# Hedgehog attention: exponents of two heads' planes side by side, keys times values as whole matmuls

## The chip, the cores and the metric

One core of a Trainium2 chip. TensorE multiplies matrices into PSUM, VectorE (DVE), ScalarE (ACT) and GpSimd (POOL) work on tiles in SBUF and (the first two) in PSUM, SyncE (SP) issues most DMAs. The metric is the device time of one execution in microseconds, as the median of several runs.

## The reference, cut to what matters

The input x (2048 rows of 512) is layer-normalised. Two branches work on the result, and both are added to x: a linear attention of 32 heads of 16 features (A), and a dense layer pair with the Mish activation (B).

```python
pq = einsum("bhsd,hdf->bhsf", q, w_phi)          # 16 features per head
pk = einsum("bhsd,hdf->bhsf", k, w_phi)
phi_q = concat([softmax(pq), softmax(-pq)])      # two planes of 16
phi_k = concat([softmax(pk), softmax(-pk)])
kv  = einsum("bhsf,bhsd->bhfd", phi_k, v)        # keys times values, over all rows
z   = einsum("bhsf->bhf", phi_k)
num = einsum("bhqf,bhfd->bhqd", phi_q, kv)
den = einsum("bhqf,bhf->bhq", phi_q, z) + 1e-6
o   = num / den
return x + o @ wo + (h * tanh(softplus(h))) @ w2   # h = xn @ w1 + b1
```

## The kernel before

The 2048 rows are 16 tiles of 128, in four groups. All instructions are issued in the order in which the code calls them (a manual schedule); every engine works through its own queue in that order, and waits come from the tiles' dependencies and from the buffers of the pools.

**First phase, four stages** (the loop over `s`, L560 to L604). Stage `s` takes the exponentials of the keys of group `s` (`exponentials`, L249, ScalarE), multiplies the keys of group `s - 1` by their values (`accumulate`, L291, TensorE), projects the values of group `s` (`value`, L176; from stage 1 on the first two tiles are copied out by VectorE, the others by ScalarE) and the logits of step `s + 1` (`logits`, L211), normalises the keys' softmaxes (`normalise`, L268, VectorE), computes hidden units of the Mish layer (`hidden`, L185: four matmuls and one ScalarE activation each), and takes the next step's maxima and minima and subtracts them (`extremes`, L219, VectorE). In stage 2 the queries' weights are folded with w_phi (`fold`, L107: 16 matmuls, four copies). In stage 0, and at the start, the loads, the layer norms and the keys' fold come first.

The exponents of a step lie in the tile `e`: per row tile two planes (one for the softmax, one for that of the negated logits) of 512 columns, 32 heads of 16 features. L242 writes a plane.

`accumulate` multiplies 32 columns of `e` (two heads, one plane) by the 33 columns of `vext` that hold these two heads' values and a one. It puts four such matmuls side by side in the array, as column tiles: 128 matmuls a group, 512 in all, into one PSUM tile `pkv` of one bank. `mask_kv` (L310, VectorE) copies it to `kvm`, and clears what belongs to the other head of each pair. `masks` (L322, POOL) prepares the mask and the constant columns of `kvm`.

**Second phase** (L607 to L702). Steps 4 to 7 are the queries' groups. They are not normalised; each tile's exponents are transposed by a DMA on SP (`turn`, L258). `attend` (L334) multiplies a tile's transposed exponents by `kvm`: 32 matmuls as four row tiles, into the four banks of `pnd`; ScalarE copies the denominators to `ds` (L357) and the numerators (L363). `combine` (L365, VectorE) forms the quotients: L379, L382, L385 and L387 work on `ds`, L394 and L401 on the numerators, and a DMA on SP transposes the outcome. `second_layer` (L412) and `project_out` (L425) are the matmuls into the output tile `po` (L420, L429); `residual` (L435) adds x on VectorE (L437), and SP stores.

**PSUM.** The eight banks are shared by pools. `ps` has four buffers and stays open. In the first phase `px` (one) is open beside it, and from the end of stage 0 on `pk` (one bank, for `pkv`) and `pz` (two). Projections, folds and hidden units take their banks in turn from these pools (`bank`, L66); the list at L602 gives the order from the last four units of stage 0 on. A matmul that opens a tile waits until the bank's former tile has been copied out. Before `attend(0, 0)` the upper four banks are given back (L614) and become `pnd`.

Of the kernel before, what the change touches and what calls it, by code (L numbers as in the profile page):

```python
# [18 lines left out]
def kernel(  # L19
# [13 lines left out]
    P = 128  # L33
# [40 lines left out]
    x_sb = persist.tile([P, NT, D], BF16, name="x_sb")  # L74
    xnT = persist.tile([P, NT, KT, P], BF16, name="xnT")
    acts = persist.tile([P, FT, S], BF16, name="acts")
    kvm = persist.tile([P, 2, 4, 36], BF16, name="kvm")
    wqk = wts.tile([P, KT, 2 * D], BF16, name="wqk")
    wsrc = wts.tile([P, 4, DH], BF16, name="wsrc")
    wv = wts.tile([P, KT, D], BF16, name="wv")  # L80
# [26 lines left out]
    def fold(wT, dst, dve, kts=range(KT)):  # L107

        for kt in kts:
            pf = bank("pfold")  # L110
            for j in range(4):
                nc.tensor.matmul(
                    pf[:, j * P : (j + 1) * P],
                    lhsT=wT[:, j, kt * P : (kt + 1) * P],
                    rhs=Wbd[:, j, :],
                    start=True,
                    stop=True,
                )
            if kt in dve:
                nc.vector.tensor_copy(dst[:, kt, :], pf[:])  # L120
            else:
                nc.scalar.copy(dst[:, kt, :], pf[:])

    def ln_stats(t0, n):

# [93 lines left out]
    def extremes(s, between=None, halves=(slice(0, TPG),)):  # L219

        if s not in e_of:
            e_of[s] = epool.tile([P, TPG, 2, 512], BF16, name="e")
        for q in halves:
            n = q.stop - q.start
            e = e_of[s][:, q]
            pv = p_of[s][:, q, :].rearrange("p t (c e) -> p (t c) e", e=16)
            for pl, op in enumerate((ALU.max, ALU.min)):
                if pl == 1 and between is not None:
                    between()
                src = pv  # L230
                for half in (8, 4, 2):
                    m = smx.tile([P, 128, half], BF16, name=f"m{half}", bufs=1)[:, 0 : n * 32, :]
                    nc.vector.tensor_tensor(  # L233
                        out=m, in0=src[:, :, 0:half], in1=src[:, :, half : 2 * half], op=op
                    )
                    src = m

                m = smx.tile([P, 128, 1, 2], BF16, name="m1", bufs=1)[:, 0 : n * 32]
                nc.vector.tensor_tensor(out=m[:, :, 0, :], in0=src, in1=src[:, :, ::-1], op=op)
                mb = m.rearrange("p (t c) u o -> p t c u o", t=n).to_broadcast([P, n, 32, 8, 2])  # L240
                p5 = pv.rearrange("p (t c) (e o) -> p t c e o", t=n, o=2)
                nc.vector.tensor_tensor(  # L242
                    out=e[:, :, pl, :].rearrange("p t (c e o) -> p t c e o", e=8, o=2),
                    in0=p5 if pl == 0 else mb,
                    in1=mb if pl == 0 else p5,
                    op=ALU.subtract,
                )

    def exponentials(s, ks=(0, 1)):  # L249
        for k in ks:  # L250
            m = 2 if s < NG else 1
            for i in range(2 * k, 2 * k + 2, m):
                v = e_of[s][:, i : i + m, :, :]
                nc.scalar.activation(v, v, ACT.Exp)  # L254
                if s >= NG:
                    turn(s, k, i)

    def turn(s, k, i):  # L258

        h = 2 * (s - NG) + k  # L260
        if i == 2 * k:
            qT_of[h] = epool.tile([P, 2, 8, P], BF16, name="qT", bufs=3)
        nc.sync.dma_start_transpose(
            out=qT_of[h][:, i - 2 * k, :, :],
            in_=e_of[s][:, i, :, :].rearrange("p l c -> p (l c)"),
        )

    def normalise(s, k, between=None):  # L268

        v = e_of[s][:, 2 * k : 2 * k + 2, :, :]  # L270
        t = smx.tile([P, 128], FP32, name="s")
        nc.vector.reduce_sum(  # L272
            t[:], v.rearrange("p t l (c e) -> p (t l c) e", e=16), axis=AX.X
        )
        if between is not None:
            between()
# [4 lines left out]
        nc.vector.tensor_copy(  # L281
            r2[:], r[:].rearrange("p (c o) -> p c o", o=1).to_broadcast([P, 128, 2])
        )
        vv = v.rearrange("p t l (c e o) -> p (t l c) e o", e=8, o=2)
        nc.vector.tensor_tensor(  # L285
            out=vv, in0=vv, in1=r2[:, :, None, :].to_broadcast([P, 128, 8, 2]), op=ALU.mult
        )
# [2 lines left out]

    def accumulate(g, pk):  # L291
        if g == 0:
            kv_of[0] = pk.tile([P, 2, 4, 33], FP32, name="pkv", tag="kv")
        e = e_of.pop(g)
        for j in range(4):
            for pl in range(2):
                for i in range(TPG):
                    for r in range(4):
                        c = j * P + 32 * r
                        nc.tensor.matmul(  # L300
                            kv_of[0][32 * r : 32 * r + 32, pl, j, :],
                            lhsT=e[:, i, pl, c : c + 32],
                            rhs=vext[g % 2][:, i, j, r, 0:33],
                            start=(g == 0 and i == 0 and j == 0 and pl == 0),
                            stop=(g == NG - 1 and i == TPG - 1),
                            skip_group_check=True,
                            tile_position=(0, 32 * r),
                        )

    def mask_kv():  # L310
        kv = kv_of[0][:].rearrange("p l j c -> p (l j) c")
        to = kvm[:].rearrange("p l j c -> p (l j) c")
        nc.vector.tensor_tensor(
            out=to[:, :, 0:32], in0=kv[:, :, 0:32],
            in1=KVmask[:, None, 0:32].to_broadcast([P, 8, 32]), op=ALU.mult,
        )
        nc.vector.scalar_tensor_tensor(
            out=to[:, :, 32:34], in0=kv[:, :, 32:33].to_broadcast([P, 8, 2]), scalar=5e-7,
            in1=KVmask[:, None, 32:34].to_broadcast([P, 8, 2]), op0=ALU.add, op1=ALU.mult,
        )  # L320

    def masks():  # L322
        for r in range(4):
            rows, own = slice(32 * r, 32 * r + 32), block[32 * r : 32 * r + 32, 2 * r : 2 * r + 2, :]
            nc.gpsimd.tensor_copy(KVmask[rows, 0:32], own.rearrange("p h d -> p (h d)"))
            nc.gpsimd.tensor_copy(KVmask[rows, 32:34], own[:, :, 0])
            nc.gpsimd.tensor_copy(
                kvm[rows].rearrange("p l j c -> p (l j) c")[:, :, 34:36],
                own[:, None, :, 0].to_broadcast([32, 8, 2]),
            )  # L330

# [2 lines left out]
    def attend(h, i):  # L334

        if i == 0:
            nd_of[h] = (
                (wkp, wv)[h % 2][:].rearrange("p (i l) c -> p i l c", i=2),
                opool.tile([P, 2, 2, 64], FP32, name="ds"),
            )  # L340
        nm, ds = nd_of[h]
        pnd = later[0].tile([P, 4, 512], FP32, name="pnd", tag="nd")
        for pl in range(2):
            for j in range(4):
                for r in range(4):
                    at, rows = (pl * 4 + j) * 36, slice(32 * r, 32 * r + 32)
                    nc.tensor.matmul(  # L347
                        pnd[:, r, at : at + 36],
                        lhsT=qT_of[h][rows, i, pl * 4 + j, :],
                        rhs=kvm[rows, pl, j, :],  # L350
                        start=True,
                        stop=True,
                        tile_position=(32 * r, 0),
                    )
        a = pnd[:, :, 0:288].rearrange("p r (l j c) -> p l j r c", l=2, j=4)
        to = nm[:, i, :, :].rearrange("p l (j r c) -> p l j r c", j=4, r=4)
        nc.scalar.copy(  # L357
            ds[:, i].rearrange("p x (g r h) -> p g r x h", g=8, r=4),
            pnd[:, :, 0:288].rearrange("p r (g c) -> p g r c", g=8)[:, :, :, 32:36].rearrange(
                "p g r (x h) -> p g r x h", x=2  # L360
            ),
        )
        nc.scalar.copy(to, a[:, :, :, :, 0:32])  # L363

    def combine(h, parts=(slice(0, 2),)):  # L365

        nm, ds = nd_of.pop(h) if parts[-1].stop == 2 else nd_of[h]
        ds = ds[:].rearrange("p i x (l c) -> p i x l c", l=2)
        if h not in oT_of:
            ob = lnp.tile([P, 4, 512], BF16, name="ob", tag="xn")  # L370
            u = opool.tile([P, 2, 2, 32], FP32, name="u")
# [5 lines left out]
        for q in parts:  # L377
            n = q.stop - q.start
            nc.vector.tensor_tensor(  # L379
                out=u[:, q], in0=ds[:, q, 0], in1=ds[:, q, 1, ::-1], op=ALU.mult  # L380
            )
            nc.vector.tensor_tensor(  # L382
                out=w[:, q], in0=u[:, q, 0, :], in1=u[:, q, 1, :], op=ALU.add
# [2 lines left out]
            for k in range(q.start, q.stop):  # L386
                nc.vector.tensor_tensor(  # L387
                    out=f[:, k],
                    in0=ds[:, k, 1, ::-1, :, None].to_broadcast([P, 2, 32, 2]),
                    in1=w[:, k, None, :, None].to_broadcast([P, 2, 32, 2]),  # L390
                    op=ALU.mult,
                )
# [167 lines left out]
    for s in range(NG):  # L560
# [33 lines left out]
        if s == 0:  # L594
# [2 lines left out]
            wide = None  # L597
            stack.close()
            pk = upper.enter_context(tc.tile_pool(name="pk", bufs=1, space=PSUM))
            pz = upper.enter_context(tc.tile_pool(name="pz", bufs=2, space=PSUM))  # L600
            hidden(6)
            turns[0] = cycle([pz, ps, ps, pz, ps, px, ps])  # L602
        hidden((4, 14, 8, 10)[s])
        extremes(s + 1)  # L604

# [127 lines left out]
```

## Time and profile before

| what | us |
|---|---|
| median of three runs | 179.92 (179.86 to 179.94) |
| profiled execution | 179.79 |
| its span, first to last instruction | 177.7 |
| TensorE busy, matmuls | 171.8 |
| VectorE busy | 153.4 |
| ScalarE busy | 125.1 |
| start of `attend(0, 0)` | 101.33 |

The profiled execution is 2.1 us longer than its span, and 0.13 us shorter than the median. In the rows below, a line such as L300 is a line of the kernel before, PE is TensorE's matmuls and PEld its weight loads. Matmuls are pipelined, so a matmul's duration is longer than its share of the engine; the step from one start to the next tells the share. Times in lists count from the span's start.

```profile
L300 PE MATMUL pkv<-vext,e 128*32 128x33 bf16 x512 | 4.8, 184 | 0.0
L347 PE MATMUL pnd<-kvm,qT 32*128 32x36 bf16 x512 | 6.0, 174 | 0.2 <-DMA qT<-e 0.2
L313 DVE TENSOR_TENSOR kvm<-pkv,KVmask 128x256 bf16<-128x256 f32 x1 | 0.4, 417 | 0.0
L317 DVE SCALAR_TENSOR_TENSOR kvm<-pkv,KVmask 128x16 bf16<-128x16 f32 x1 | 0.2, 165 | 0.0
```

These are groups of equal instructions: line, engine, operation, output and inputs, shapes, count, then busy time in us, the mean duration in ns, and idle time before them with what ended it.

### The profile page before, as it was taken

Reading aid. Unit: us, or ns where it says so; the run is one execution under the profiler, and the core shown is the slowest. Engines: PE = TensorE matmul, PEld = TensorE weight load, DVE = VectorE, ACT = ScalarE, POOL = GpSimd, SP = SyncE. Lnnn points to the kernel's source line nnn. Section 1 sums busy time; section 2 is a strip of 40 time slices with the busy share of each in tenths; the row PEclk is TensorE's granted clock in tenths of the full one; section 3 lists DMA queues with packets and bytes.
Section 4 is the critical chain, followed back from the end, with each engine's and each line's share of the span. In section 5 each row is a group of like instructions: output and inputs, shape, how many; then the busy total and the mean of one; then the engine's idle time right before and its main releaser. Section 6 shows DMA issues by size and latency. Waiting matters only on the chain.

```text
span 177.7 us, 4351 instructions
## 1 busy us (share of the span) xinstructions
PE 171.8 (97%) x1806; PEld 81.7 (46%) x1806; DVE 153.4 (86%) x304; ACT 125.1 (70%) x174; POOL 28.5 (16%) x40
## 2 busy tenths in 40 slices
PE   6799999999999999999999999999999999999993
PEld 2444444454444545554454444444444444444561
DVE  1989699999999989998999979789889978789943
ACT  3667999997998799969994899389223863543200
POOL 5203029900699400000000000000000000000000
PEclk9999999999999999999999999999999999999999
DMA  6998793330013600000000693909956098394343
GB/s 143 283 400 303 144 367 140 59 65 0 4 39 73 128 0 0 4 4 0 0 0 4 127 119 67 108 8 180 198 123 91 7 168 96 89 122 120 64 107 129
DMA packets 44560, 18.13 MB, mean 102 GB/s; under 512 B 36988, under 2 KB 44028, under 8 KB 44540
## 3 DMA queue, kind: packets, MB, share of 16 engines
q1 hardware_dynamic: 43568, 17.50, 45.8%
q10 hardware_dynamic: 972, 0.35, 0.7%
q8 instruction: 14, 0.23, 0.5%
q14 instruction: 6, 0.05, 0.1%
HBM read 6.84 MB, written 2.10 MB: 50 GB/s over the span
## 4 chain that ended last, share of the span: by engine, by line
DVE 47%; PE 43%; DMA 4%; ACT 2%; issue 2%; DVEq 0%
PE po L420 23%; DVE s L272 10%; PE pproj L170 8%; PE po L429 6%; DVE m L233 6%; DVE e L285 6%; DVE e L242 6%; DVE r L280 4%; PE ph L191 3%; DVE stats L130 3%; ACT e L254 2%; PE pnd L347 2%; DMA qT<-e 2%; DMA x_sb<-in_A_x_dram 2%; DVE r L281 2%
## 5 line engine op out<-in xcount | busy, mean ns | idle before, releaser
L420 PE MATMUL po<-w_sb,acts 128*128 128x512 bf16 (+1 forms) x238 | 51.0, 367 | 0.4 <-DVE x_sb L437 0.4
L191 PE MATMUL ph<-xnT,w_sb 128*128 128x512 bf16 x224 | 49.5, 379 | 0.0
L254 ACT ACTIVATE e<-e 128x1024 bf16<-128x1024 bf16 (+1 forms) x24 | 30.8, 1338 | 7.9 <-DVE e L242 7.8
L204 ACT ACTIVATE acts<-ph,b1f 128x512 bf16<-128x512 f32 x56 | 34.3, 706 | 1.5 <-PE ph L191 1.4
L191 PEld LDWEIGHTS <-w_sb 128*128 128x128 bf16 x224 | 21.9, 98 | 26.4 <-issue 0.3
L420 PEld LDWEIGHTS <-acts 128*128 128x128 bf16 x238 | 22.2, 98 | 22.8 <-issue 0.3
L170 PEld LDWEIGHTS <-xnT 128*128 128x128 bf16 x192 | 18.2, 97 | 22.0 <-issue 1.2
L272 DVE TENSOR_REDUCE s<-e 128x128 f32<-128x2048 bf16 x8 | 18.2, 2273 | 1.6 <-ACT e L254 1.6
L142 POOL TENSOR_SCALAR xn<-x_sb,mv,rstd 128x512 bf16<-128x512 bf16 x8 | 16.6, 2080 | 0.2
L437 DVE TENSOR_TENSOR x_sb<-po,x_sb 128x512 bf16<-128x512 f32 (+1 forms) x17 | 10.9, 658 | 6.1 <-PE po L429 6.1
L357 ACT COPY ds<-pnd 128x128 f32<-128x128 f32 x16 | 4.4, 274 | 16.2 <-PE pnd L347 15.7
L170 PE MATMUL pproj<-wv,xnT 128*128 128x512 bf16 x64 | 15.0, 380 | 0.0
L429 PE MATMUL po<-wqk,ob 128*128 128x512 bf16 (+1 forms) x68 | 15.0, 367 | 0.0
L233 DVE TENSOR_TENSOR m<-m 128x256 bf16<-128x256 bf16 (+2 forms) x44 | 13.4, 305 | 1.5
L170 PE MATMUL pproj<-wqk,xnT 128*128 128x512 bf16 x64 | 14.5, 379 | 0.0
L217 ACT CAST p_sb<-pproj 128x512 bf16<-128x512 f32 x20 | 10.7, 586 | 3.4 <-PE pproj L170 1.8
L170 PE MATMUL pproj<-wkp,xnT 128*128 128x512 bf16 x52 | 12.6, 379 | 0.2
L285 DVE TENSOR_TENSOR e<-e,r 128x2048 bf16<-128x2048 bf16 x8 | 10.7, 1336 | 0.3
L233 DVE TENSOR_TENSOR m<-p_sb 128x1024 bf16<-128x1024 bf16 (+1 forms) x18 | 10.2, 564 | 0.0
L429 PEld LDWEIGHTS <-ob 128*128 128x128 bf16 x68 | 6.5, 98 | 6.8 <-DMA ob<-ob 0.3
L242 DVE TENSOR_TENSOR e<-p_sb,m 128x2048 bf16<-128x2048 bf16 (+1 forms) x9 | 8.9, 989 | 0.3
L242 DVE TENSOR_TENSOR e<-m,p_sb 128x2048 bf16<-128x2048 bf16 (+1 forms) x9 | 8.9, 988 | 0.3
(73 smaller groups left out, 174.0 us busy)
## 6 DMA issues: line engine op xcount, KB each, us to landing
w_sb<-in_B_w_dram SPq DMA_DIRECT2D x2, 1792.0 KB, 8.6
out_dram<-x_sb SPq DMA_DIRECT2D x15, 128.0 KB, 1.9
x_sb<-in_A_x_dram SPq DMA_DIRECT2D x1, 1024.0 KB, 11.4
x_sb<-in_A_x_dram SPq DMA_DIRECT2D x1, 512.0 KB, 4.3
wv<-in_A_wqkv_dram SPq DMA_DIRECT2D x1, 512.0 KB, 4.9
wqk<-in_A_wo_dram SPq DMA_DIRECT2D x1, 512.0 KB
x_sb<-in_A_x_dram SPq DMA_DIRECT2D x1, 256.0 KB, 3.2
x_sb<-in_A_x_dram ACTq DMA_DIRECT2D x1, 256.0 KB, 3.4
```

The source lines that it names most:

```text
L142: engine.tensor_scalar(out=xn[:, at + i, :], in0=x_sb[:, t0 + i, :], scalar1=mv[:, i, 0:1], scalar2=rstd[:, i : i + 1], op0=ALU.subtract, ...
L170: nc.tensor.matmul(pp, lhsT=xnT[:, t, kt, :], rhs=w[:, kt, :], start=(kt == 0), stop=(kt == KT - 1),)
L191: nc.tensor.matmul(ph[:], lhsT=w1_sb[:, kt, f * P : (f + 1) * P], rhs=xnT[:, g * TPG : (g + 1) * TPG, kt, :], start=(kt == 0), stop=(kt == ...
L204: nc.scalar.activation(acts[:, f, g * 512 : (g + 1) * 512], ph[:], ACT.Mish, bias=b1f[:, f : f + 1])
L233: nc.vector.tensor_tensor(out=m, in0=src[:, :, 0:half], in1=src[:, :, half : 2 * half], op=op)
L242: nc.vector.tensor_tensor(out=e[:, :, pl, :].rearrange("p t (c e o) -> p t c e o", e=8, o=2), in0=p5 if pl == 0 else mb, in1=mb if pl == 0 ...
L254: nc.scalar.activation(v, v, ACT.Exp)
L272: nc.vector.reduce_sum(t[:], v.rearrange("p t l (c e) -> p (t l c) e", e=16), axis=AX.X)
L285: nc.vector.tensor_tensor(out=vv, in0=vv, in1=r2[:, :, None, :].to_broadcast([P, 128, 8, 2]), op=ALU.mult)
L420: nc.tensor.matmul(po[:, c], lhsT=acts[:, f, t * P : (t + 1) * P], rhs=w2_sb[:, f, c], start=(f == 0), stop=False,)
L429: nc.tensor.matmul(po[:, c], lhsT=oT_of[h][:, t % 2 * 4 + j, :], rhs=wo_sb[:, j, c], start=False, stop=(j == 3),)
L437: nc.vector.tensor_tensor(out=y, in0=po[:, c], in1=y, op=ALU.add)
```

## The change

The planes of a tile of `e` are interleaved: 16 blocks of two heads, each with its 32 columns of the first plane and its 32 of the second. The folds' copies also permute the blocks, so that block pair `b` holds heads 2b, 2b + 1 and 16 + 2b, 17 + 2b. So 128 neighbouring columns of `e` hold both planes of two pairs of heads.

`accumulate` takes these 128 columns as one matmul's weights, and the 66 columns of `vext` that belong to the two pairs as its moving operand: 32 matmuls a group instead of 128, with no column tiles. `pkv` has 8 x 128 words a row, two banks; half of what it computes belongs to the other pair and is not read. `mask_kv` has four instructions instead of two, each on 64 rows. `pz` has one buffer instead of two, and the order of banks has six places instead of seven.

In `attend` the 32 matmuls stand in another order, `kvm` is indexed by block, and the four columns of denominators are ordered so that `ds` holds for each plane 32 pairs of words; L379 and L387 then read every second word of `ds`. The copies to `ds` and of the numerators have the same number of elements.

```diff
@@ fold
-            if kt in dve:
-                nc.vector.tensor_copy(dst[:, kt, :], pf[:])
-            else:
-                nc.scalar.copy(dst[:, kt, :], pf[:])
+            copy = nc.vector.tensor_copy if kt in dve else nc.scalar.copy
+            copy(
+                dst[:, kt, :].rearrange("p (b a c) -> p a b c", b=8, a=2),
+                pf[:].rearrange("p (a b c) -> p a b c", a=2, b=8),
+            )
@@ extremes
-            e_of[s] = epool.tile([P, TPG, 2, 512], BF16, name="e")
+            e_of[s] = epool.tile([P, TPG, 16, 2, 32], BF16, name="e")
...
-                    out=e[:, :, pl, :].rearrange("p t (c e o) -> p t c e o", e=8, o=2),
+                    out=e[:, :, :, pl, :].rearrange("p t b (h e o) -> p (t b) h e o", h=2, o=2),
@@ accumulate
-            kv_of[0] = pk.tile([P, 2, 4, 33], FP32, name="pkv", tag="kv")
+            kv_of[0] = pk.tile([P, 8, 128], FP32, name="pkv", tag="kv")
         e = e_of.pop(g)
-        for j in range(4):
-            for pl in range(2):
-                for i in range(TPG):
-                    for r in range(4):
-                        c = j * P + 32 * r
-                        nc.tensor.matmul(
-                            kv_of[0][32 * r : 32 * r + 32, pl, j, :],
-                            lhsT=e[:, i, pl, c : c + 32],
-                            rhs=vext[g % 2][:, i, j, r, 0:33],
-                            start=(g == 0 and i == 0 and j == 0 and pl == 0),
-                            stop=(g == NG - 1 and i == TPG - 1),
-                            skip_group_check=True,
-                            tile_position=(0, 32 * r),
-                        )
+        for b in range(8):
+            for i in range(TPG):
+                nc.tensor.matmul(
+                    kv_of[0][:, b, 0:66],
+                    lhsT=e[:, i, 2 * b : 2 * b + 2].rearrange("p a l c -> p (a l c)"),
+                    rhs=vext[g % 2][:, i, b // 4 :: 2, b % 4, 0:33],
+                    start=(g == 0 and i == 0 and b % 4 == 0),
+                    stop=(g == NG - 1 and i == TPG - 1),
+                    skip_group_check=True,
+                )
@@ mask_kv
+        for r in range(2):
+            rows = slice(64 * r, 64 * r + 64)
+            kv, to, h = kv_of[0][rows, :, 33 * r : 33 * r + 33], kvm[rows], KVmask[rows]
...
@@ attend
-                opool.tile([P, 2, 2, 64], FP32, name="ds"),
+                opool.tile([P, 2, 2, 32, 2], FP32, name="ds"),
...
-                        pnd[:, r, at : at + 36],
+                    pnd[:, r % 2 * 2 + r // 2, 36 * b : 36 * b + 36],
...
@@ combine
-                out=u[:, q], in0=ds[:, q, 0], in1=ds[:, q, 1, ::-1], op=ALU.mult
+                out=u[:, q], in0=ds[:, q, :, :, 0], in1=ds[:, q, ::-1, :, 1], op=ALU.mult
...
-                    in0=ds[:, k, 1, ::-1, :, None].to_broadcast([P, 2, 32, 2]),
+                    in0=ds[:, k, ::-1, :, 1, None].to_broadcast([P, 2, 32, 2]),
@@ end of stage 0
-            pz = upper.enter_context(tc.tile_pool(name="pz", bufs=2, space=PSUM))
+            pz = upper.enter_context(tc.tile_pool(name="pz", bufs=1, space=PSUM))
             hidden(6)
-            turns[0] = cycle([pz, ps, ps, pz, ps, px, ps])
+            turns[0] = cycle([pz, ps, ps, px, ps, ps])
```

More of the change, by code (lines that the diff above doesn't have):

```diff
@@ L76 @@
     acts = persist.tile([P, FT, S], BF16, name="acts")
-    kvm = persist.tile([P, 2, 4, 36], BF16, name="kvm")
+    kvm = persist.tile([P, 8, 36], BF16, name="kvm")
     wqk = wts.tile([P, KT, 2 * D], BF16, name="wqk")
@@ L239, in extremes @@
                 nc.vector.tensor_tensor(out=m[:, :, 0, :], in0=src, in1=src[:, :, ::-1], op=op)
-                mb = m.rearrange("p (t c) u o -> p t c u o", t=n).to_broadcast([P, n, 32, 8, 2])
-                p5 = pv.rearrange("p (t c) (e o) -> p t c e o", t=n, o=2)
+                mb = m.rearrange("p (b h) u o -> p b h u o", h=2).to_broadcast([P, n * 16, 2, 8, 2])
+                p5 = pv.rearrange("p (b h) (e o) -> p b h e o", h=2, o=2)
                 nc.vector.tensor_tensor(
-                    out=e[:, :, pl, :].rearrange("p t (c e o) -> p t c e o", e=8, o=2),
+                    out=e[:, :, :, pl, :].rearrange("p t b (h e o) -> p (t b) h e o", h=2, o=2),
                     in0=p5 if pl == 0 else mb,
@@ L252, in exponentials @@
             for i in range(2 * k, 2 * k + 2, m):
-                v = e_of[s][:, i : i + m, :, :]
+                v = e_of[s][:, i : i + m].rearrange("p t b l c -> p (t b l c)")
                 nc.scalar.activation(v, v, ACT.Exp)
@@ L264, in turn @@
             out=qT_of[h][:, i - 2 * k, :, :],
-            in_=e_of[s][:, i, :, :].rearrange("p l c -> p (l c)"),
+            in_=e_of[s][:, i].rearrange("p b l c -> p (b l c)"),
         )
     def normalise(s, k, between=None):
-        v = e_of[s][:, 2 * k : 2 * k + 2, :, :]
+        v = e_of[s][:, 2 * k : 2 * k + 2].rearrange("p t b l c -> p (t b l c)")
         t = smx.tile([P, 128], FP32, name="s")
         nc.vector.reduce_sum(
-            t[:], v.rearrange("p t l (c e) -> p (t l c) e", e=16), axis=AX.X
+            t[:], v.rearrange("p (c e) -> p c e", e=16), axis=AX.X
         )
@@ L283, in normalise @@
         )
-        vv = v.rearrange("p t l (c e o) -> p (t l c) e o", e=8, o=2)
+        vv = v.rearrange("p (c e o) -> p c e o", e=8, o=2)
         nc.vector.tensor_tensor(
@@ L310, in mask_kv @@
-    def mask_kv():
[L311 to L320, printed above, removed]
+        for b in range(8):
[8 more added lines that the diff above has]
+                )
@@ new lines, in mask_kv @@
+    def mask_kv():
+        for r in range(2):
+            rows = slice(64 * r, 64 * r + 64)
+            kv, to, h = kv_of[0][rows, :, 33 * r : 33 * r + 33], kvm[rows], KVmask[rows]
+            nc.vector.tensor_tensor(
+                out=to[:, :, 0:32], in0=kv[:, :, 0:32],
+                in1=h[:, None, 0:32].to_broadcast([64, 8, 32]), op=ALU.mult,
+            )
+            nc.vector.scalar_tensor_tensor(
+                out=to[:, :, 32:36:2], in0=kv[:, :, 32:33].to_broadcast([64, 8, 2]), scalar=5e-7,
+                in1=h[:, None, 32:34].to_broadcast([64, 8, 2]), op0=ALU.add, op1=ALU.mult,
+            )
@@ L327, in masks @@
             nc.gpsimd.tensor_copy(
-                kvm[rows].rearrange("p l j c -> p (l j) c")[:, :, 34:36],
+                kvm[rows, :, 33:36:2],
                 own[:, None, :, 0].to_broadcast([32, 8, 2]),
@@ L342, in attend @@
         pnd = later[0].tile([P, 4, 512], FP32, name="pnd", tag="nd")
[L343 to L347, printed above, removed]
-                        pnd[:, r, at : at + 36],
[L349 to L356, printed above, removed]
+        for b in range(8):
+            for r in range(4):
+                rows = slice(32 * r, 32 * r + 32)
+                nc.tensor.matmul(
+                    pnd[:, r % 2 * 2 + r // 2, 36 * b : 36 * b + 36],
+                    lhsT=qT_of[h][rows, i, b, :],
+                    rhs=kvm[rows, b, :],
+                    start=True,
+                    stop=True,
+                    tile_position=(32 * r, 0),
+                )
+        a = pnd[:, :, 0:288].rearrange("p a (b c) -> p a b c", b=8)
         nc.scalar.copy(
[L358 to L361, printed above, removed]
-        )
-        nc.scalar.copy(to, a[:, :, :, :, 0:32])
+            ds[:, i].rearrange("p l (a b h) x -> p (l a) b (h x)", a=2, b=8), a[:, :, :, 32:36]
+        )
+        nc.scalar.copy(
+            nm[:, i, :, :].rearrange("p l (a b c) -> p (l a) b c", a=2, b=8), a[:, :, :, 0:32]
+        )
     def combine(h, parts=(slice(0, 2),)):
         nm, ds = nd_of.pop(h) if parts[-1].stop == 2 else nd_of[h]
-        ds = ds[:].rearrange("p i x (l c) -> p i x l c", l=2)
         if h not in oT_of:
```

## The prediction

> **What bounds the kernel now.** I read the page's first two parts, then the chain that ended last in order of time, then TensorE's timeline around the work that the change touches.
>
> ```profile
> PE 171.8 (97%) x1806; PEld 81.7 (46%) x1806; DVE 153.4 (86%) x304; ACT 125.1 (70%) x174; POOL 28.5 (16%) x40
> ...
> DVE  1989699999999989998999979789889978789943
> ```
>
> TensorE is never idle for long, VectorE hardly. The chain says which of the two sets the time, stage by stage.
>
> ```profile
> 95.69 1.24 DVE e L242
> ...
> 97.91 0.12 ACT e L254
> 98.03 3.26 DMA qT<-e
> 101.28 0.05 issue
> 101.33 0.37 PE pnd L347 x32
> ...
> 164.31 0.61 DVE x_sb L437
> 164.92 0.04 issue
> 164.97 6.24 PE po L420 x42
> ```
>
> From 22 to 97 us the chain is VectorE (reduce, reciprocal, scale, maxima, subtraction) but for two exponentials of ScalarE's at 61.83 and 79.38, then one more exponential and one transposing DMA, and at 101.33 `attend(0, 0)` starts. From there to 155 it is TensorE alone, then VectorE to 164.9, then TensorE. So what happens before 101.33 counts only if it moves that start. TensorE is almost as late there as the DMA:
>
> ```profile
> 91.33 0.38 PE L191 MATMUL ph<-xnT,w_sb 128*128 128x512 bf16 x1
> 91.64 1.20 PE L300 MATMUL pkv<-vext,e 128*32 128x33 bf16 x128
> 92.77 3.63 PE L170 MATMUL pproj<-wqk,xnT 128*128 128x512 bf16 x16
> 96.23 3.18 PE L420 MATMUL po<-w_sb,acts 128*128 128x512 bf16 x14
> 99.25 1.89 PE L191 MATMUL ph<-xnT,w_sb 128*128 128x512 bf16 x8
> 101.33 0.37 PE L347 MATMUL pnd<-kvm,qT 32*128 32x36 bf16 x32 [0.19 <-DMA qT<-e]
> ```
>
> Columns: start, duration, instruction, count. Matmuls overlap, so I read steps between starts: 3.02 us for 14 matmuls of 512 columns is 0.216 each. The eight of L191 fill 99.25 to 100.98; a change of tiling shows 0.09 more before the first tiled matmul (91.33 + 0.216 = 91.54, first L300 at 91.64). TensorE could start `attend` at 101.07: **its slack is 0.26 us**. A gain of TensorE's before this place is lost in this wait; a loss shows beyond 0.26.
>
> **The change, part by part.**
>
> *Keys times values.* Before, one `accumulate` takes 91.54 to 92.77, 1.23 us, drains at both ends included; the one at 74.86 reads the same. It becomes 32 matmuls of 128 rows, 128 features and 66 columns, without a change of tiling. No row has 66 columns. The row of 128 columns, with the same 128x128 weights:
>
> ```profile
> 66.97 1.06 PE L112 MATMUL pfold<-Wbd,wT 128*128 128x128 bf16 x16
> 67.86 0.38 PE L191 MATMUL ph<-xnT,w_sb 128*128 128x512 bf16 x1
> ```
>
> 0.89 us for 16: 55.6 ns. With 216 ns at 512 columns that is 0.417 ns a column, so 66 columns give 29.8 ns. Bounds: 55.6 ns above; below, the L347 matmuls, whose 32 starts lie 6.5 ns apart: four row tiles, which together load 128 columns of weights on all rows and stream 36 columns, take 25.8 ns. That row also says that loading 128 columns of weights can recur every 26 ns, so I take 29.8: 32 x 29.8 = 0.95 us, 0.28 less per `accumulate` (ends: 0.83 and 1.78 us, that is 0.40 less to 0.55 more).
>
> The Trainium skill (TensorE: Matmul & The Clock Gate, LDWEIGHTS) speaks against this: it gives a weight load as columns / 1.2 ns, 107 ns for 128. By it an `accumulate` would be an estimated 3.4 us. The trace disagrees so far: folds recur every 55.6 ns, load and matmul together.
>
> *One bank less for everything else.* `pkv` takes two banks, `pz` one instead of two. From 35 us on, projections, folds and hidden units rotate over six banks instead of seven, so a tile's first matmul needs the copy out of the tile six before, not seven. I set each tile's start against the end of the copy six tiles earlier. It bites where ScalarE is late, behind the exponentials:
>
> ```profile
> 79.38 3.71 ACT L254 ACTIVATE e<-e 128x2048 bf16<-128x2048 bf16 x2 [1.64 <-DVE e L242]
> 83.00 2.02 ACT L217 CAST p_sb<-pproj 128x512 bf16<-128x512 f32 x4
> ...
> 83.00 0.56 ACT L217 CAST p_sb<-pproj 128x512 bf16<-128x512 f32 x1
> ...
> 82.91 0.81 PE L191 MATMUL ph<-xnT,w_sb 128*128 128x512 bf16 x3
> ```
>
> In stage 3 the order is two values (VectorE copies), four logits, two values (ScalarE copies), ten hidden units. The first unit, at 82.91, had the bank of the second value, free since 80.54. Now it gets that of the first logits, whose copy ends at 83.56; with the 0.05 that pass at 164.92 between release and matmul, it starts at **83.61**. In stage 2 (four folds before the units) the first unit, at 67.86, needs the third value's copy (67.34 to 67.96): 68.01. In stage 1 it needs a copy that ends at 45.92, 0.77 ahead of its start at 46.69: no wait. The later units have 0.1 us or more once the first has slipped.
>
> Running TensorE forward: minus 0.28 after `accumulate(0)`, minus 0.56 after `accumulate(1)`; at 68.01 the lead is gone and it is 0.15 late; `accumulate(2)` makes that minus 0.13; the start at 83.61 is 0.70 late; `accumulate(3)` leaves 0.42. It is ready for `attend` at 101.07 + 0.42 = 101.49 instead of 101.33, **0.17 us later** with rounding; the DMA at 101.28 no longer decides. ScalarE's units in stage 3 run from 87.31 without waiting for TensorE (the first unit's matmuls would end at 84.6), so the exponentials and VectorE's chain do not move.
>
> *The layout of e.* Maxima, reduce, reciprocal, scale and exponential keep their shapes. L242 writes runs of 32 elements instead of 512. Nearest row: L233, whose reads already step over runs of 8 elements, takes 682 ns for 1024 elements, like L242 with 1024 unbroken (692). So 0. Ends: nothing shows a gain, but a run's length could price either way; a loss goes up to the rate of the reduce, 2273 ns for 2048 against 1226.
>
> *Fold copies.* Eight copies write runs of 32. VectorE's copies of values, which do, take 682 against 681 ns; ScalarE's 607 against 586. So 0.02 us for one head copy that TensorE waits for: 0 to 0.06 over three, and the four in stage 2 lie in ScalarE's queue 0.6 us ahead of need.
>
> *mask_kv.* Two more VectorE instructions, on 64 rows but with the same elements per row: 0.42 + 0.17 = 0.58 us more, from 96.8. They come after the last subtraction that `attend(0)` needs. Behind them wait three logits copies (97.24 to 99.12), whose banks the hidden units need at 99.25 and 100.11 (free then at 98.5 and 99.1), the maxima of step 5, and `combine(0)`; VectorE idles 0.55 before L379 at 105.81, which takes up all but 0.03 us. `kvm` is ready near 98.0, 3 us early. Without that cover it would cost the 0.58.
>
> *attend and combine.* The same 512 matmuls in another order, the same 128 and 1024 elements in ScalarE's copies (274 and 1018 ns). L379 and L387 read every second word of `ds`. No row prices that: ends are 0 and twice the element time. I take 0, since L317 reads words 33 apart at 165 ns for 16, no more than L540's 173 for 14 side by side. Order and sizes of all DMAs on SP, and POOL's work, stay.
>
> **Sum:** 0.17 us on the profiled execution's 179.79 is 179.96. The median shown is 0.13 above that execution: 180.1. From 179.92 no change can be told within 0.2%, 0.36 us, so the forecast is no change.
>
> **Rivals.**
>
> 1. *Slower: the whole matmuls do not reach 30 ns*, because weights and columns do not overlap so well with short matmuls. Each ns adds 0.032 to an `accumulate`. After the stall of stage 3 only the last one counts: 0.70 late, minus its gain, minus the slack of 0.26. It decides from 36 ns on (gain below 0.08). At 45 ns: 0.65, 180.6; at 55.6 all four count: 4 x 0.55 - 0.26 = 1.94, 181.9. For it: no row has short whole matmuls. Against: 25.8 ns at L347.
> 2. *Slower: each short matmul waits for its own weight load.* The loads of L112 and L191 last 98 ns: 32 x 98 = 3.14 us, 1.91 more per `accumulate`, 4 x 1.91 - 0.26 = 7.4: 187.3. Against: the folds' loads last as long and recur every 55.6 ns. By the Trainium skill's 107 ns (TensorE: Matmul & The Clock Gate, LDWEIGHTS) it would be an estimated 8.5 more, 188.4.
> 3. *The six banks cost nothing*, because the stall is shorter than read. Then TensorE comes early and the DMA at 101.28 decides as before: 179.9.
> 4. *Slower: combine on strided words.* From 155.3 to 164.9 VectorE is the chain; L379 for 256 elements and L387 for 512. A further 64 elements of L379 take 69 ns (216 to 285), so twice the element time adds 0.28 + 0.55 = 0.83, on top of the 0.17: 180.9 to 181.0. Against: L317, above.
> 5. *Slower: the subtraction at the reduce's rate.* Eight full-size L242 lie on the chain, 1.05 more each: 188.3. Against: L233, whose broken reads cost nothing.
> 6. *Faster: the same eight come out shorter.* The chain up to 101.28 and ScalarE's copy at 83.56 move together; it takes 0.53 over eight, 66 ns each of 1226, to pass 0.2%: 179.3 to 179.56. Nothing in the rows shows it.
>
> **How the numbers follow.** Forecast 0.45, case 3 0.05 (both no change: 0.50); case 1 0.25, case 2 0.02, case 4 0.08, case 5 0.03 (slower: 0.38); case 6 0.12. The range 179.5 to 181.0 leaves out cases 2 and 5, the part of case 1 above 47 ns (0.07) and half of case 6: 0.18.
>
> **What would show it.** The 32 matmuls of an `accumulate` 30 ns apart, with no gap before or after. A wait of TensorE's for a ScalarE copy of 0.8 us at the first hidden unit of stage 3, a smaller one in stage 2. The first transposed exponentials landing still near 101.3, and the first `attend` matmul 0.2 later with no wait for it. L242 at 1226, L379 at 216 and L387 at 290 ns. The forecast is wrong if the spacing is above 36 ns, if L242 changes, or if TensorE waits for banks at other places too.

## The result and the profile after

| | before | after |
|---|---|---|
| median, us | 179.81 | 180.14 |
| profiled execution, us | 179.79 | 179.97 |
| its span, us | 177.7 | 177.9 |
| start of `attend(0, 0)`, us | 101.33 | 101.52 |

The ratio is 1.002, interval 1.0014 to 1.0027: 0.33 us slower, 0.25 to 0.49, right at the 0.2% below which the prediction spoke of no change.

In the kernel after, line numbers differ: L298 is `accumulate`'s matmul (before L300), L192 the hidden unit's (L191), L218 the logits' copy (L217), L344 `attend`'s (L347), L414 the second layer's (L420), L243 the subtraction (L242), L373 and L381 are `combine`'s first lines (L379, L387).

The chain that ended last, after, in order of time (start, duration, engine and line):

```profile
78.11 1.24 DVE e L243
...
81.19 1.89 ACT e L255
83.08 0.48 ACT p_sb L218
83.56 0.04 issue
83.60 8.79 PE ph L192 x40
92.40 0.99 PE pkv L298 x32
93.39 3.45 PE pproj L171 x16
96.84 3.02 PE po L414 x14
99.86 1.73 PE ph L192 x8
101.59 0.31 PE pnd L344 x32
```

Before, VectorE carried this chain to 97 us and a DMA brought it to `attend`. Now it leaves VectorE at 79 us, runs through ScalarE's second exponential and the copy of the first logits, and from 83.60 it is TensorE without a break. The step from ScalarE to TensorE is the wait for a bank. TensorE's timeline around the first hidden unit of stage 3 and to the start of `attend`:

```profile
81.73 1.24 PE L171 MATMUL pproj<-wv,xnT 128*128 128x512 bf16 x5
83.60 0.59 PE L192 MATMUL ph<-xnT,w_sb 128*128 128x512 bf16 x2 [0.63 <-ACT p_sb L218]
...
92.23 1.16 PE L298 MATMUL pkv<-vext,e 128*128 128x66 bf16 x32
93.23 3.62 PE L171 MATMUL pproj<-wqk,xnT 128*128 128x512 bf16 x16
...
99.70 1.89 PE L192 MATMUL ph<-xnT,w_sb 128*128 128x512 bf16 x8
101.52 0.37 PE L344 MATMUL pnd<-kvm,qT 32*128 32x36 bf16 x32
```

The hidden unit starts at 83.60, before at 82.91. The brackets count only time in which nothing ran; between starts the wait is 0.80 us (from 82.59, the start of the last matmul before it, to 83.60, less the 0.216 of a step). `accumulate(3)` takes 92.23 to 93.23, 0.99 us, before 1.23: it gives 0.24 back. The first matmul of `attend` has no bracket any more: the transposed exponentials landed at 101.25, TensorE came at 101.52.

### The profile page after: what moved, and what is told of

It is laid out like the page before. It is cut to its first block, busy times and chain, and to the rows that moved or that the text cites. A ratio compares the mean times of both kernels' runs of the same rounds, so it can differ in the third digit from the quotient of the medians.

```text
span 177.9 us, 3585 instructions
## 1 busy us (share of the span) xinstructions
PE 171.4 (96%) x1422; PEld 81.7 (46%) x1422; DVE 154.0 (87%) x306; ACT 125.0 (70%) x174; POOL 28.5 (16%) x40
## 4 chain that ended last, share of the span: by engine, by line
PE 53%; DVE 37%; ACT 3%; issue 2%; DMA 2%; DVEq 0%
PE po L414 25%; PE pproj L171 10%; PE ph L192 9%; DVE s L273 7%; PE po L423 6%; DVE e L286 5%; DVE m L234 5%; DVE e L243 4%; DVE r L281 3%; DVE stats L131 3%; ACT e L255 2%; PE pnd L344 2%; DMA x_sb<-in_A_x_dram 2%; DVE r L282 1%; DVE x_sb L431 1%
## 5 line engine op out<-in xcount | busy, mean ns | idle before, releaser
L414 PE MATMUL po<-w_sb,acts 128*128 128x512 bf16 (+1 forms) x238 | 51.0, 367 | 0.4 <-DVE x_sb L431 0.4
L192 PE MATMUL ph<-xnT,w_sb 128*128 128x512 bf16 x224 | 49.5, 379 | 0.8 <-ACT p_sb L218 0.6
L192 PEld LDWEIGHTS <-w_sb 128*128 128x128 bf16 x224 | 21.9, 98 | 27.4 <-issue 1.4
L414 PEld LDWEIGHTS <-acts 128*128 128x128 bf16 x238 | 22.2, 98 | 22.8 <-issue 0.3
L218 ACT CAST p_sb<-pproj 128x512 bf16<-128x512 f32 x20 | 10.7, 586 | 3.4 <-PE pproj L171 1.8
L243 DVE TENSOR_TENSOR e<-p_sb,m 128x2048 bf16<-128x2048 bf16 (+1 forms) x9 | 8.9, 989 | 0.3
L243 DVE TENSOR_TENSOR e<-m,p_sb 128x2048 bf16<-128x2048 bf16 (+1 forms) x9 | 8.9, 989 | 0.3
```

The costliest lines, as they stand in the source:

```text
L192: nc.tensor.matmul(ph[:], lhsT=w1_sb[:, kt, f * P : (f + 1) * P], rhs=xnT[:, g * TPG : (g + 1) * TPG, kt, :], start=(kt == 0), stop=(kt == ...
L243: nc.vector.tensor_tensor(out=e[:, :, :, pl, :].rearrange("p t b (h e o) -> p (t b) h e o", h=2, o=2), in0=p5 if pl == 0 else mb, in1=mb i ...
L414: nc.tensor.matmul(po[:, c], lhsT=acts[:, f, t * P : (t + 1) * P], rhs=w2_sb[:, f, c], start=(f == 0), stop=False,)
```

## The experiments

### What the lost bank costs alone

The kernel before, with one bank less in the order and nothing else of the change:

```diff
-            pz = upper.enter_context(tc.tile_pool(name="pz", bufs=2, space=PSUM))
+            pz = upper.enter_context(tc.tile_pool(name="pz", bufs=1, space=PSUM))
...
-            turns[0] = cycle([pz, ps, ps, pz, ps, px, ps])
+            turns[0] = cycle([pz, ps, ps, px, ps, ps])
```

> The kernel before with one edit of the change alone: pz with one buffer and the bank order of six places. The column tiles, the layout of e and the one-bank pkv stay. My theory (the lost bank costs TensorE a wait of 0.7 us in stage 3, and the shorter matmuls give back only the last accumulate's share): TensorE waits near 82.9 us for the copy of the first logits that ends near 83.56 and starts at 83.61; with the old accumulate it is ready for the first attend at 101.07 + 0.70 = 101.77 instead of 101.33, so the time goes up by 0.44 us, more than the whole change's 0.33. Rival (the lost bank is harmless, the new matmuls or copies cost the time): no wait at 82.9, no change within 0.1 us.

Measured: 180.47 us against 179.90, ratio 1.0028, interval 1.0017 to 1.0039: slower by 0.50 us by the ratio, 0.57 by the medians. TensorE's timeline:

```profile
83.90 0.59 PE L191 MATMUL ph<-xnT,w_sb 128*128 128x512 bf16 x2 [0.40 <-ACT p_sb L217]
...
100.24 1.89 PE L191 MATMUL ph<-xnT,w_sb 128*128 128x512 bf16 x8
102.06 0.37 PE L347 MATMUL pnd<-kvm,qT 32*128 32x36 bf16 x32
```

The same wait at the same tile, and `attend` starts without waiting for the DMA. This execution's first phase ran 0.29 us late from its head on (its first reduce starts at 25.71, before at 25.42); counted from there the start is 0.44 later than before, as expected. So the lost bank alone makes TensorE late, and the rival falls. That it costs more than the whole change is not shown by the times, whose intervals overlap (1.0014 to 1.0027 for the change). The profiles show it: counted from the first reduce, `attend` starts after 76.36 us here, after 76.11 in the kernel after. The difference of 0.25 is about what `accumulate(3)` gives back (0.24).

### What the rest of the change costs without the lost bank

The changed kernel with 64 columns per matmul, so that `pkv` fits one bank, and with two buffers of `pz` and the old order of seven. It leaves out the sums of the keys' features, and so the denominators; `mask_kv` keeps its four instructions and reads other columns instead.

```diff
-            kv_of[0] = pk.tile([P, 8, 128], FP32, name="pkv", tag="kv")
+            kv_of[0] = pk.tile([P, 8, 64], FP32, name="pkv", tag="kv")
...
-                    rhs=vext[g % 2][:, i, b // 4 :: 2, b % 4, 0:33],
+                    rhs=vext[g % 2][:, i, b // 4 :: 2, b % 4, 0:32],
...
-            pz = upper.enter_context(tc.tile_pool(name="pz", bufs=1, space=PSUM))
+            pz = upper.enter_context(tc.tile_pool(name="pz", bufs=2, space=PSUM))
...
-            turns[0] = cycle([pz, ps, ps, px, ps, ps])
+            turns[0] = cycle([pz, ps, ps, pz, ps, px, ps])
```

> The changed kernel with 64 columns per matmul instead of 66, so that pkv fits one bank, and with two buffers of pz and the bank order of seven places again. It leaves out the sums of the keys' features (the columns of ones), so the denominators are not computed. Everything else of the change stays. My theory: no wait of TensorE's for banks in stage 3; TensorE comes about a microsecond early to the first attend and waits there for the transposed exponentials, so the start is at 101.25 to 101.35 and the time is that of the kernel before, within 0.1 us: the gain of the matmuls (4 x 0.24) is lost in that wait. Rival 1 (the layout, the masks or the strided words cost the 0.33 us): it stays 0.3 us slower than before. Rival 2 (TensorE's time sets the end): about 0.9 us faster than before.

Measured: 179.94 us against 179.90, ratio 0.9998, interval 0.9989 to 1.0007. TensorE's waits between 60 and 103 us:

```profile
PE pnd L344 <- DMA qT<-e: 0.5, 1, 0.5
PE ph L192 <- ACT p_sb L218: 0.3, 1, 0.3
```

The time is that of the kernel before: both rivals fall, and layout, masks and strided words cost nothing that can be seen. TensorE is early at `attend` and waits 0.54 us for the DMA. The start, 101.49, lies outside my 101.25 to 101.35 because this execution's head was late (first reduce at 25.70); counted from there it is 75.80, in the profile of the kernel before 75.91. But I had expected no waits for banks. There are two, 0.1 us at the first hidden unit of stage 2 and 0.3 at the second of stage 3 (0.27 and 0.48 between starts): a TensorE that runs 0.6 to 0.7 us ahead meets ScalarE's copies with seven banks too. So it came 0.6 us early, not a full microsecond.

### Taking the wait away by moving work

The changed kernel; in stage 3 ScalarE copies the logits between the two exponentials.

```diff
-        exponentials(s, (0, 1) if s else (0,))
+        exponentials(s, (0, 1) if s in (1, 2) else (0,))
...
             for i in range(TPG):
                 logits(s + 1, i, act)
+            if s == 3:
+                exponentials(3, (1,))
```

> The changed kernel with one move in stage 3: ScalarE copies the four logits tiles after the first of the stage's two exponentials instead of after the second. Nothing is added or removed. My theory: the first logits' bank is free near 81.8 instead of 83.56, TensorE does not wait at the first hidden unit of stage 3 and is ready for attend near 100.8; the start is set by the DMA again, 101.25 to 101.35, 0.2 us earlier than in the changed kernel, and the time equals the kernel before within 0.15 us. The second exponential ends near 85.1, and the reduce that needs it starts at 86.2, so VectorE does not notice. Rival (the wait in stage 3 is only a symptom): the wait goes and the time stays 0.3 us above before.

Measured: 179.85 us against 179.90, ratio 0.9999, interval 0.9990 to 1.0008. ScalarE's timeline in stage 3:

```profile
79.54 1.91 ACT L255 ACTIVATE e<-e 128x2048 bf16<-128x2048 bf16 x1 [1.64 <-DVE e L243]
81.36 2.03 ACT L218 CAST p_sb<-pproj 128x512 bf16<-128x512 f32 x4
83.25 1.94 ACT L255 ACTIVATE e<-e 128x2048 bf16<-128x2048 bf16 x1
```

TensorE's, at the first hidden unit of stage 3 and at `attend`:

```profile
82.97 1.46 PE L192 MATMUL ph<-xnT,w_sb 128*128 128x512 bf16 x6
...
101.40 0.37 PE L344 MATMUL pnd<-kvm,qT 32*128 32x36 bf16 x32 [0.38 <-DMA qT<-e]
```

The copies begin at 81.36 instead of 82.99, the unit at 82.97 has no bracket, and `attend` waits for the DMA again. Its start, 101.40, is a little above the 101.35 that I had allowed, again by a late head (first reduce at 25.55, so 75.85 from there). The same instructions in another order undo the whole loss: the wait in stage 3 is its cause.

### The kernel before once more, and the one after

> The kernel before once more, for a second profile. In the first profile the DMA that sets the start of attend landed 0.26 us after TensorE could have started. The medians differ by 0.33 us, the two profiled executions by 0.18. My theory: the landing moves by a tenth or so from one execution to the next, and where it lands earlier only the kernel before gains by it, so here the landing (or the start) differs from 101.33 by up to 0.2 us while TensorE's own readiness stays at 101.07. Rival: the start is the same to 0.02 us, and the difference between 0.33 and 0.18 is from other places.

A single execution, 179.62 us. The DMA landed at 101.10 and `attend` started at 101.15; TensorE's readiness, which I had expected to stay at 101.07, was at 100.91. So readiness moved as well, and the slack is 0.24 us here against 0.26: the whole first phase shifts with its head. VectorE's timeline shows the first reduce of this profile, which starts at 25.42 in the first:

```profile
25.32 2.26 DVE L272 TENSOR_REDUCE s<-e 128x128 f32<-128x2048 bf16 x1
```

Counted from that reduce, `attend` starts after 75.83 us here and 75.91 in the first profile: of the difference 0.10 us is the head's, and 0.08 is the landing's. (Such differences are taken from unrounded times.)

> The changed kernel once more. Its profiled execution was 0.18 us above that of the kernel before, its median 0.33 us (interval 0.25 to 0.49). My theory: the places named give 0.19 to 0.24 us, and the rest is scatter between executions, so this series lies at 0.1 to 0.35 us above before, and the profile shows the same wait of 0.6 to 0.8 us at the first hidden unit of stage 3. Rival (something that the first profile did not show adds 0.1 us or more): 0.3 us or more again.

Measured: 180.11 us against 179.83, ratio 1.0017, interval 1.0008 to 1.0026; the wait at the hidden unit of stage 3 is 0.64. It does not decide between theory and rival by the times: 0.28 us by the medians, 0.31 by the ratio, and the interval of 0.14 to 0.47 reaches into both. The starts counted from the first reduce do more: 76.11 and 76.15 in the two profiles after, 75.91 and 75.83 before. The means are 0.26 apart, so the named places explain 0.26 of the 0.28 to 0.33. From `attend` to the end all four profiles take the same 76.37 to 76.38 us. What is left is within the intervals; whether it is scatter stays open.

### The order of the short matmuls

The two loops of `accumulate` exchanged:

```diff
-        for b in range(8):
-            for i in range(TPG):
+        for i in range(TPG):
+            for b in range(8):
```

> The changed kernel with the two loops of accumulate exchanged: the row tile outside, the block inside, so that no two neighbouring matmuls add to the same columns of PSUM. It asks what sets the step of the whole matmuls, 30 ns with every eighth at 36 and another at 33. My theory: the columns streamed set it, so the step stays at 30 ns and an accumulate at 0.98 to 1.0 us. Rival (adding to the columns just written delays it): all steps at 30 or below, 0.96 us or less.

One execution, 180.22 us. An `accumulate` takes 0.99 to 1.00 us in both orders. Most steps between starts are 30 ns; the longer ones (32 to 37) fall on other matmuls. So the rival falls: adding to the columns just written is not what delays. What makes the longer steps stays open. With 64 columns (the experiment with one bank) it took 0.94.

### What the shorter matmuls are worth where TensorE is late

If the gain is lost in the wait for VectorE's chain, it must come back when that chain is shortened. Four kernels test it. The halves, in both kernels (here the changed one):

```diff
-            m = 2 if s < NG else 1
+            m = 1 if s >= NG or (s >= 2 and k == 0) else 2
...
-        nc.vector.reduce_sum(
-            t[:], v.rearrange("p (c e) -> p c e", e=16), axis=AX.X
-        )
+        w = 64 if s >= 2 and k == 0 else 128
+        for q in range(0, 128, w):
+            nc.vector.reduce_sum(
+                t[:, q : q + w],
+                v.rearrange("p (c e) -> p c e", e=16)[:, q : q + w, :],
+                axis=AX.X,
+            )
```

In the last two, also the copies between the exponentials of stage 3 (above), and the fold of stage 2 behind its hidden units:

```diff
-        if s == 2:
-            fold(wT, wqp, ())
...
         hidden((4, 14, 8, 10)[s])
+        if s == 2:
+            fold(wT, wqp, ())
```

Before, with halves:

> The kernel before with VectorE's chain made shorter: in stages 2 and 3 the first exponential is taken in two halves of 1024, and the first reduce in two halves, so that VectorE begins about 0.8 us earlier in each of the two stages. Nothing of the change is in it. My theory: the transposed exponentials land about 1.6 us earlier, near 99.7, but TensorE is ready for attend only at 101.07, so the start comes 0.26 us earlier and no more: 0.2 to 0.3 us faster than before. Rival (VectorE's chain still sets the start, or TensorE has room that I do not see): 1 us or more faster. Other rival (the halves cost what they win): no change.

After, with halves:

> The changed kernel with the same two halves in stages 2 and 3. My theory: ScalarE's copies of stage 3 come 0.7 us earlier too (the first logits near 82.9 instead of 83.56), so the wait for a bank there all but goes, and TensorE is ready near 100.85; it and not the DMA sets the start: 0.4 to 0.55 us faster than before, 0.7 faster than the changed kernel, and faster than the kernel before with the same halves. Rival (the change's matmuls are worth nothing even then): the same time as the kernel before with the halves.

After, with all three edits:

> The changed kernel with the halves, with the logits copies of stage 3 between its exponentials, and with the fold of the queries' weights moved behind the eight hidden units of stage 2. Nothing is left out. My theory: no wait of TensorE's for a bank is left, so all of the four accumulates' gain (4 x 0.24) arrives: TensorE is ready near 100.1, the transposed exponentials land near 99.7 to 100, and the time is 0.9 to 1.3 us below before: 178.6 to 179.0. Rival (another wait takes the place, in ScalarE's queue most likely): 0.5 us or less.

Before, with all three edits:

> The kernel before with the same three edits (halves, logits copies between the exponentials of stage 3, fold behind the hidden units). My theory: it had no waits for banks, so only the halves count and TensorE with its old accumulates is ready at 101.07: 0.2 to 0.3 us faster than before. The difference to the changed kernel with the same edits is what the whole matmuls are worth where TensorE sets the start, about 0.9 us. Rival: both gain alike, and the whole matmuls are worth nothing.

| kernel | us | ratio to before | interval | DMA landed | TensorE ready | first reduce |
|---|---|---|---|---|---|---|
| before, halves | 179.63 | 0.9985 | 0.9977 to 0.9994 | 99.97 | 101.35 | 25.75 |
| after, halves | 179.50 | 0.9977 | 0.9968 to 0.9985 | 100.02 | 101.25 | 25.82 |
| before, all | 179.55 | 0.9984 | 0.9976 to 0.9993 | 99.87 | 101.28 | 25.68 |
| after, all | 178.70 | 0.9932 | 0.9921 to 0.9944 | 99.75 | 100.14 | 25.46 |

(Before in these runs: 179.86.) The last three columns are from the profiled executions. The DMA lands 1.2 to 1.4 us before TensorE is ready in the first three: VectorE's chain is out of the way. The heads of these three were 0.27 to 0.40 us later than the first profile's, so the columns compare only from the first reduce on: there the kernel before is ready after 75.59 us with the halves and with all edits, and after 75.65 and 75.59 in its two profiles without. It gains 0.23 to 0.31 us, about the slack of 0.26, and no more from all three edits. The changed kernel with the halves alone gains 0.36 by the medians and 0.41 by the ratio, at the lower edge of my 0.4 to 0.55. Its interval and that of before with the halves overlap, so that it beats that one is not shown by the times (counted from the first reduce it is ready 0.16 earlier). Its wait in stage 3 is gone, but in stage 2 two folds and the first hidden unit still wait for ScalarE's copies, 0.27 us each between starts; that is what moving the fold takes away. With all three edits it gains 1.16 us, where I had expected 0.9 to 1.3. Its chain that ended last, from 79 us on:

```profile
78.89 3.45 PE pproj L171 x16
82.34 8.67 PE ph L192 x40
91.01 0.99 PE pkv L302 x32
92.01 3.45 PE pproj L171 x16
95.46 3.02 PE po L418 x14
98.48 1.73 PE ph L192 x8
100.21 0.31 PE pnd L348 x32
```

TensorE alone, no step to another engine. Counted from the first reduce `attend` starts 0.92 us earlier than before with the same edits (74.68 against 75.60): the four accumulates' 4 x 0.24 = 0.95, nearly all of it. This version is faster than both kernels.

## Why the prediction was right

- **What bounds the kernel.** Right: TensorE's slack of a quarter of a microsecond against the DMA decided what counted. The kernel before with halves gained about that slack (0.23 by the medians, interval 0.11 to 0.41).
- **Keys times values.** The mechanism was right, the size a little off. The sum took 29.8 ns a matmul from the rows of 512 and 128 columns, 0.95 us in all; it was 31.1 ns and 0.99 us:

```profile
L298 PE MATMUL pkv<-vext,e 128*128 128x66 bf16 x128 | 4.6, 193 | 0.0
L298 PEld LDWEIGHTS <-e 128*128 128x128 bf16 x128 | 4.5, 97 | 0.9
```

  (Groups of equal instructions, after: busy time, mean ns of one, idle time before.) A load lasts 97 ns, but loads recur every 31: rival 2 is out. The Trainium skill's figure (TensorE: Matmul & The Clock Gate, LDWEIGHTS: columns / 1.2 ns, 107 for 128) is not far from the 97 that one load lasts; as a price per matmul, which gave the prediction's estimates of 3.4 us an `accumulate` and of 188.4 us in all, the trace disagrees. Rival 1 would have needed 36 ns.
- **One bank less.** Right for stage 3, in place and size: 83.61 was forecast and 83.60 measured. In stage 2 the time was right, 68.01 forecast and 68.00 measured, but a place was missed. TensorE's timeline after:

```profile
66.43 1.46 PE L112 MATMUL pfold<-Wbd,wT 128*128 128x128 bf16 x16
68.00 0.81 PE L192 MATMUL ph<-xnT,w_sb 128*128 128x512 bf16 x3
```

  The 16 matmuls of the folds take 1.57 us to the next start, before 0.89. The third and the fourth fold wait too, 0.14 and 0.27 us between starts, each until a copy of logits by ScalarE has ended; the unit then waits 0.27. The prediction named waits at other places as a sign that it is wrong. It had set the starts of before against the copies, though TensorE comes to the folds 0.53 us earlier after the change. The folds' waits cost nothing here, because the unit's bank came free last. The method, each tile's start against the end of the copy as many tiles back as there are banks, needed only the trace of before. Rival 3 falls. The Trainium skill (Perfetto Trace Analysis, Optimization Strategy) says that repeated bubbles on the engine that should be saturated can mean too little PSUM. The trace agrees: three small ones in stage 2 and a large one in stage 3, each ending about 0.05 us after a ScalarE copy.
- **The start of attend.** 101.49 was forecast, 101.52 measured; the 0.03 is the 31.1 ns, less gain in `accumulate(3)`. (The prediction's own terms, 0.42 less the slack of 0.26, give 0.16, not 0.17.)
- **Layout, strided words, mask_kv.** Right. The subtraction and the first line of `combine`, after (L243, L373) and before (L242, L379):

```profile
L243 DVE TENSOR_TENSOR e<-m,p_sb 128x2048 bf16<-128x2048 bf16 x5 | 6.1, 1226 | 0.2
L242 DVE TENSOR_TENSOR e<-m,p_sb 128x2048 bf16<-128x2048 bf16 x5 | 6.1, 1225 | 0.2
L373 DVE TENSOR_TENSOR u<-ds 128x64 f32<-128x64 f32 x12 | 2.6, 217 | 0.0
L379 DVE TENSOR_TENSOR u<-ds 128x64 f32<-128x64 f32 x12 | 2.6, 218 | 0.5 <-ACT ds L357 0.5
```

  L381 takes 291 ns (L387 before: 291), and ScalarE's copies of the folds 588 and 658 (587 and 655), so the 0.02 us for them did not come. ScalarE's copy to `ds` went from 274 to 265 ns, without effect. `mask_kv` put the logits copies 0.68 us later (97.92 instead of 97.24), a little over the 0.58, and the second L373 of `combine(0)` starts at 105.99 instead of 105.81: the idle 0.55 took it up but for TensorE's own 0.19. Rivals 4 and 5 fall, and nothing of rival 6 was seen.
- **The sum.** 0.17 was forecast on the profiled execution, 0.18 came; the medians differ by 0.33, interval 0.25 to 0.49, so 0.17 is too small. The start after was forecast well. What was off is the start of before that is subtracted, 101.33, read from one execution. Counted from the first reduce, its DMA landed after 75.87 us, the latest of the eight profiles in which VectorE's chain was left as it is (the others: 75.75 to 75.84), and only a kernel whose TensorE is early waits for that landing. The two profiles of each kernel put the shift of the start at 0.26; the rest stays open. That the profiled executions differ by just 0.18, and that 180.14 came where 180.1 was forecast, is partly luck: the profiled execution after was the fastest of its 19, and 180.1 was counted from a median of before of 179.92, which is 179.81 over more runs. "No change" holds only just: the interval reaches across 0.2%.

## What to carry to other kernels

When a change takes a buffer from a ring, set each tile's start against the release of the tile one place nearer; the first negative difference gives the place and the size of the wait, and here it hit where the releasing engine had been away on something long. Use the starts of the new kernel, with what it has gained by then: with the old ones, two waits were missed here. Where two chains end within a few tenths of a microsecond of each other, a gain on one is worth only the slack, and a loss on it counts in full beyond the slack; the gain has to be bought out by shortening the other chain too. Moving the copies that free banks ahead of a long instruction that nobody needs yet took the loss away here, and cost nothing that can be seen.

## What was not expected

The whole first phase starts up to half a microsecond earlier or later from one execution to the next: its first reduce began between 25.32 and 25.82 us in the twelve profiles of this study. Starts are better compared counted from such a mark than from the span's start. And four column tiles of 33 columns recur every 32 ns here (8.0 ns from start to start), one whole matmul with the weights of all four and 66 columns every 31: at these sizes the tiles save no time on TensorE, and a change of tiling costs 0.09 us before and 0.1 us after in addition (38.33 + 0.22 = 38.54 against the first L300 at 38.64; the last at 39.65, the next whole matmul at 39.77). So of the 0.24 us that an `accumulate` gains, about 0.2 are the two changes of tiling that it no longer has, and only 0.03 the matmuls themselves.
